# Feed-forward products that take their columns pair by pair in another order, in five of eight chunks

## The chip, the cores and the metric

The kernel runs on one core of a Trainium2 chip. The metric is the device time of one execution in microseconds. Five engines work side by side: TensorE (PE, with its weight loads shown as PEld), VectorE (DVE), ScalarE (ACT), GpSimd (POOL), and SyncE (SP), which issues all DMAs here.

## The reference

Block-local attention with summary keys, followed by a feed-forward layer without a bias. Batch 4, 8 heads, 768 positions, head size 64; model width 512, inner width 2048, 3072 tokens.

```python
k_sum = k.reshape(B, H, nb, 32, D).max(axis=3)
v_sum = v.reshape(B, H, nb, 32, D).mean(axis=3)
scores_l = np.where(abs(pos_q - pos_k) < 16, scale * q @ k.T, -1e9)
scores_s = scale * q @ k_sum.T + log(32)
a = softmax(concatenate([scores_l, scores_s]))
x = (a @ concatenate([v, v_sum])).transpose(0, 2, 1, 3).reshape(3072, 512)
h = x @ w_in
g = where(h >= 1, h, where(h <= -1, 0, (h + 1) ** 2 / 4))
out = g @ w_out
```

## The kernel before

The 3072 tokens are worked in 8 chunks (c) of 384. For each chunk, attention for 4 pairs of heads (p) gives `x` turned: four tiles of 128 model columns by 384 tokens. To keep accuracy, every operand of the feed-forward products is split into a high and a low part in a rounded 32-bit format: `xhi`, `xlo` for `x`, `ghi`, `glo` for the gated inner layer, and `halves` for the weights, whose tiles stay in SBUF for the whole kernel. A product is then three matmuls: high by low, low by high, high by high.

The inner width is walked in 16 steps (f) of 128 columns. A step has these parts:

- `ff1` (L302): 4 pieces (k) of the model width by 3 matmuls, 12 in all, each with 128x128 weights as the stationary operand and 384 token columns of `xhi` or `xlo` as the moving one. All 12 add into one PSUM tile `h` (pool `ps_h`, two buffers).
- the gate (L311 to L329), on ScalarE, VectorE and GpSimd, which writes `ghi` and `glo`.
- `ff2` (L331): 3 groups (i) of 128 tokens by 3 matmuls, 9 in all, with 128x128 of `ghi` or `glo` as the stationary operand and 512 columns of the second weights (`halves`) as the moving one. They add into three PSUM tiles `acc`, one bank each, over all 16 steps.

At the end of a chunk the three `acc` tiles are copied out (L341) and stored (L349).

Chunk 0, with the loading and conversion of the weights, follows an order written out by hand (`OPENING`). From chunk 1 on, a loop gives the order on TensorE: in each step the 12 matmuls of `ff1`, then the 9 of `ff2` of two steps earlier (`LAG` = 2), and every fourth step parts of the attention of the next chunk (scores, transposes, values) between them. The two last `ff2` steps of a chunk fall behind the first `ff1` steps of the next. The other engines follow the waits that result from it.

Of the kernel before, what the change touches and what calls it, by code (L numbers as in the profile page):

```python
# [19 lines left out]
P = 128  # L20
# [7 lines left out]
T = 384  # L28
# [31 lines left out]
FIRST = [[("k", 2), ("q", 2)], [("k", 3), ("q", 3)], [("kraw", 1), ("vraw", 1)], [("kraw", 2), ("vraw", 2)],  # L60
         [("kraw", 3), ("vraw", 3)], [("v", 2), ("v", 3)], [("q", 0), ("q", 1)]]
K_COPY = "vgvg"
HI_POOL = [0, 1, 2, 3, 4, 5, 6, 7, 8, 9, 10, 11, 12, 13, 14, 15]


@with_exitstack
def fused_kernel(ctx: ExitStack, tc: tile.TileContext, q2, kT, kwin, vT, vwin, w_in, w_out, mask, ident, out):
    nc = tc.nc
# [19 lines left out]
    weight, raws, converting, halves = {}, {}, {}, {}  # L88

    def room(i, what, shape, dtype):  # L90

        return wpool.tile(shape, dtype, tag=f"w{i}", name=f"{what}{i}")
# [39 lines left out]
    def convert_high(i):  # L132
        halves[i] = room(i, "halves", [P, 2, 2 * DM], F32R)
        if i in HI_POOL:
            nc.gpsimd.tensor_copy(out=halves[i][:, 0], in_=converting[i].bitcast(F32))
# [13 lines left out]
    def input_tile(pool, what, shape, c, p):  # L149
        if c == 0 and (what, p) in at_first:  # L150
            return at_first[what, p]
        tag, bufs = ("w", W_BUFS) if pool is stage else (what, {"k": K_BUFS, "q": Q_BUFS, "v": 2}[what])
        return pool.tile(shape, F32, tag=tag, name=f"{what}{c}_{p}", bufs=bufs)
# [45 lines left out]
    def window_keys(c, p):  # L199

        k_t = k_ts[c, p] = input_tile(load, "k", [P, NB, KA], c, p)
        eng = {"v": nc.vector, "g": nc.gpsimd}[K_COPY[p]]
        blocks = raws["k", p].rearrange("p (n q) -> p n q", q=QB)
# [95 lines left out]

    hs, ts, gs, acc, outs = {}, {}, {}, {}, {}  # L300

    def ff1(c, f, k):  # L302
        if k == 0:
            hs[c, f] = ps_h.tile([P, 512], F32, tag="h", name=f"h{c}_{f}")
        x_hi, x_lo = xs[c, k]
        for n, (w, x) in enumerate(((1, x_hi), (0, x_lo), (0, x_hi))):
            nc.tensor.matmul(hs[c, f][:, :T], weight["win", f][w][:, k * P:(k + 1) * P], x,  # L307
                             start=(k == 0 and n == 0), stop=(k == NK - 1 and n == 2))


# [20 lines left out]
    def ff2(c, f):  # L331
        if f == 0:
            acc[c] = [ps.tile([P, DM], F32, tag="ps", name=f"acc{c}_{i}") for i in range(NTT)]
        g_hi, g_lo = gs[c, f]
        for i in range(NTT):
            rows = slice(i * P, (i + 1) * P)
            for n, (a, w) in enumerate(((g_lo, 0), (g_hi, 1), (g_hi, 0))):
                nc.tensor.matmul(acc[c][i], a[:, rows], weight["wout", f][w], start=(f == 0 and n == 0),  # L338
                                 stop=(f == NF - 1 and n == 2))

    def result(c, i):  # L341
# [11 lines left out]
    def load_constants():  # L353
# [9 lines left out]
        "T": transposes, "P": turned, "Y": sum_vals, "Z": turn_vals, "V": mean_vals, "W": spread_vals, "A": values, "X": high, "L": low,  # L363
        "a": convert_top, "b": convert_low, "c": convert_join, "d": convert_high, "e": convert_rest,
        "F": ff1, "G": gate_half, "H": gate_square, "I": gate_min, "J": gate_high, "O": gate_rest, "B": ff2, "U": result, "o": store,
    }
    done = set()
# [118 lines left out]
```

## Time and profile before

| | |
|---|---|
| median of 3 runs | 670.58 us (668.12 to 671.68) |
| span of the profiled execution | 670.7 us; no separate time is recorded beside it |
| instructions | 11802 |
| mean granted TensorE clock | 0.982 |
| matmuls of the first product (L307) | 1536, 192 per chunk |
| matmuls of the second product (L338) | 1152, 144 per chunk |

A matmul's duration as shown includes the time in which it overlaps the one before and after it, so the pace of TensorE is read from the distance between starts, or from the chain of waits, not from the mean duration. The trace names tiles without their numbers: `h`, `acc`, `xhi`, `halves` stand for all chunks, and the chunk is found by the time.

### The profile page before, as it was taken

The page shows a single profiled execution, that of the slowest core. Times are in us where ns is not written, and L with a number is a line of the kernel's source. Part 1 is how long each engine was busy: PE and PEld are TensorE (multiplying, and loading weights), DVE is VectorE, ACT ScalarE, POOL GpSimd, SP SyncE. Part 2 cuts the span into 40 slices and gives each one's busy share as a digit, 9 for nine tenths or more (in the row PEclk, how much of TensorE's full clock was granted, in tenths as well). Part 3 has the DMA queues.
Part 4 walks back from the last instruction along what each step waited for, and adds up shares of the span by engine and source line. Part 5 has one row for each costly group of instructions (what it writes and reads, how often), then busy time and mean ns, then how long its engine had stood idle before and what let it go on. Part 6 is the DMA issues. An engine that isn't in the chain of part 4 may idle for free.

```text
span 670.7 us, 11802 instructions
## 1 busy us (share of the span) xinstructions
PE 633.5 (94%) x4448; PEld 559.4 (83%) x4448; DVE 259.4 (39%) x561; ACT 367.5 (55%) x945; POOL 267.1 (40%) x300
## 2 busy tenths in 40 slices
PE   2579998779999999999999999999999999999997
PEld 2478986668888888988888889888888988889996
DVE  5899974642233321245322322336222322311111
ACT  3889745555555545555554554555545645544332
POOL 2589996333332333234333333334233333322221
PEclk9789999879999999999999999999999999999999
DMA  8999703851111401154111311135110200000001
GB/s 285 311 354 323 250 1 85 248 145 52 53 52 53 145 19 35 52 169 124 53 53 48 106 45 52 52 112 181 53 42 11 88 19 19 1 17 32 1 1 47
DMA packets 49768, 63.56 MB, mean 95 GB/s; under 512 B 24880, under 2 KB 33328, under 8 KB 49712
## 3 DMA queue, kind: packets, MB, share of 16 engines
q1 hardware_dynamic: 49712, 62.81, 30.9%
q8 instruction: 35, 0.57, 0.4%
q14 instruction: 21, 0.17, 0.1%
HBM read 56.51 MB, written 6.29 MB: 94 GB/s over the span
## 4 chain that ended last, share of the span: by engine, by line
PE 82%; DMA 7%; ACT 4%; DVE 4%; issue 2%; POOL 1%; SPq 0%; ACTq 0%; DVEq 0%; POOLq 0%
PE h L307 36%; PE acc L338 36%; PE o_ps L286 4%; PE s_ps L242 3%; DMA raw<-in_w_out 3%; PE t_ps L275 3%; DMA raw<-in_w_in 2%; DMA kraw<-in_kT 1%; ACT e L260 1%; DMA first<-in_vT 1%; DMA first<-in_kT 1%; ACT raw L110 1%; DVE c L124 1%; DVE w L130 1%; DVE c L127 1%
## 5 line engine op out<-in xcount | busy, mean ns | idle before, releaser
L307 PE MATMUL h<-xhi,halves 128*128 128x384 f32 x1024 | 285.4, 341 | 5.6 <-DVE t L319 5.5
L338 PE MATMUL acc<-halves,ghi 128*128 128x512 f32 x768 | 240.2, 394 | 0.0
L329 POOL TENSOR_TENSOR glo<-t,ghi 128x384 fp32r<-128x384 f32 x128 | 129.3, 1013 | 200.6 <-ACT ghi L324 194.5
L307 PEld LDWEIGHTS h<-xhi,halves 128*128 128x128 f32 x1024 | 188.5, 189 | 14.1 <-DVE t L319 4.8
L319 DVE SCALAR_TENSOR_TENSOR t<-h,t 128x384 f32<-128x384 f32 x128 | 70.8, 557 | 280.7 <-ACT t L316 268.9
L307 PE MATMUL h<-xlo,halves 128*128 128x384 f32 x512 | 173.3, 338 | 0.0
L338 PEld LDWEIGHTS acc<-halves,ghi 128*128 128x128 f32 x768 | 145.1, 189 | 27.9
L338 PE MATMUL acc<-halves,glo 128*128 128x512 f32 x384 | 154.2, 401 | 0.0
L313 ACT ACTIVATE t<-h,ones_half 128x384 f32<-128x384 f32 x128 | 73.6, 578 | 130.5 <-PE h L307 120.0
L260 ACT ACTIVATE e<-e,den 128x120 f32<-128x120 f32 x192 | 73.3, 383 | 63.8 <-DVE den L255 63.8
L324 ACT CAST ghi<-t 128x384 fp32r<-128x384 f32 x128 | 65.3, 513 | 64.5 <-DVE t L319 64.0
L307 PEld LDWEIGHTS h<-xlo,halves 128*128 128x128 f32 x512 | 96.8, 189 | 4.3 <-DVE xlo L297 0.4
L338 PEld LDWEIGHTS acc<-halves,glo 128*128 128x128 f32 x384 | 72.5, 189 | 12.3 <-issue 1.0
L270 POOL TENSOR_TENSOR e<-e,den 128x360 f32<-128x360 f32 x64 | 49.8, 790 | 61.6 <-DVE den L266 55.8
L316 ACT ACTIVATE t<-t 128x384 f32<-128x384 f32 x128 | 66.8, 525 | 3.7
L214 POOL COPY k<-ks 128x144 f32<-128x144 f32 x30 | 9.2, 310 | 86.4 <-DMA k<-in_kwin 61.1
L143 POOL TENSOR_TENSOR halves<-w,halves 128x1024 fp32r<-128x1024 f32 x16 | 38.6, 2415 | 0.9
L230 POOL COPY v<-v 24x640 f32<-24x640 f32 x30 | 21.5, 717 | 39.7 <-issue 37.2
L286 PEld LDWEIGHTS o_ps<-pt,v 120*64 120x64 f32 x720 | 25.0, 144 | 13.8 <-ACT ghi L324 7.5
L297 DVE TENSOR_TENSOR xlo<-o_ps,xhi 128x384 fp32r<-128x384 f32 x32 | 17.7, 554 | 47.3 <-ACT xhi L292 47.3
L260 ACT ACTIVATION_READ_ACCUMULATOR e<-e,den 128x1 f32 x192 | 35.9, 187 | 0.0
L275 PE MATMUL t_ps<-ident_sb,e 128*120 128x128 f32 x192 | 30.8, 298 | 5.2 <-POOL e L270 5.0
(56 smaller groups left out, 426.4 us busy)
## 6 DMA issues: line engine op xcount, KB each, us to landing
k<-in_kwin SPq DMA_DIRECT2D x28, 360.0 KB, 4.3
v<-in_vwin SPq DMA_DIRECT2D x30, 288.0 KB, 3.1
raw<-in_w_in SPq DMA_DIRECT2D x16, 512.0 KB, 10.8
raw<-in_w_out SPq DMA_DIRECT2D x16, 512.0 KB, 11.0
out<-o SPq DMA_DIRECT2D x24, 256.0 KB, 2.1
q<-in_q SPq DMA_DIRECT2D x56, 96.0 KB, 4.0
kraw<-in_kT SPq DMA_DIRECT2D x13, 384.0 KB, 3.8
vraw<-in_vT SPq DMA_DIRECT2D x13, 384.0 KB, 3.8
```

The lines of the kernel that those rows point to most:

```text
L143: nc.gpsimd.tensor_tensor(out=lo, in0=converting[i].bitcast(F32), in1=hi.bitcast(F32), op=ALU.subtract)
L260: nc.scalar.activation(out=e[:, t, :], in_=e[:, t, :], func=AF.Exp, bias=nm[:, t:t + 1], scale=1.0, accum_out=den[:, t:t + 1])
L270: nc.gpsimd.tensor_tensor(out=e, in0=e, in1=den.unsqueeze(2).broadcast_to([P, NT, KA]), op=ALU.mult)
L275: nc.tensor.transpose(t_pss[c, p, j][:KA, t * P:(t + 1) * P], es[c, p, j][:, t, :], ident_sb)
L286: nc.tensor.matmul(o_pss[c, p][j * D:(j + 1) * D, cols], v_ts[c, p][:KA, blk, j * D:(j + 1) * D], pts[c, p, j][:KA, cols], start=True, sto ...
L307: nc.tensor.matmul(hs[c, f][:, :T], weight["win", f][w][:, k * P:(k + 1) * P], x, start=(k == 0 and n == 0), stop=(k == NK - 1 and n == 2))
L313: nc.scalar.activation(out=ts[c, f], in_=hs[c, f][:, :T], func=AF.Relu, bias=ones_half, scale=0.5)
L316: nc.scalar.square(out=ts[c, f], in_=ts[c, f])
L319: nc.vector.scalar_tensor_tensor(out=ts[c, f], in0=hs[c, f][:, :T], scalar=1.0, in1=ts[c, f], op0=ALU.max, op1=ALU.min)
L324: nc.scalar.copy(out=hi, in_=ts[c, f])
L329: nc.gpsimd.tensor_tensor(out=lo, in0=ts[c, f], in1=hi.bitcast(F32), op=ALU.subtract)
L338: nc.tensor.matmul(acc[c][i], a[:, rows], weight["wout", f][w], start=(f == 0 and n == 0), stop=(f == NF - 1 and n == 2))
```

## The change

In chunks 2, 3 and 4 the matmuls of `ff1`, and in chunks 5 and 6 those of `ff2`, take the columns of their moving operand in another order, and write them to PSUM in the same other order, so every sum lands where it did before. The columns are cut into `count` equal blocks; pairs of two adjacent columns stay together, and the matmul takes the first pair of every block, then the second pair of every block, and so on.

| chunk | product | blocks | distance from one pair to the next |
|---|---|---|---|
| 2 | `ff1`, 384 columns | 2 | 192 columns (768 bytes), then back |
| 3 | `ff1` | 24 | 16 columns (64 bytes) |
| 4 | `ff1` | 12 | 32 columns (128 bytes) |
| 5 | `ff2`, 512 columns | 32 | 16 columns (64 bytes) |
| 6 | `ff2` | 2 | 256 columns (1024 bytes), then back |

A column is one 4-byte value in each partition. Stationary operands, waits, buffers and the order of the instructions on every engine stay as they are; the same number of matmuls stands in the same places, with shapes such as 128x96x2x2 in place of 128x384.

```diff
+STRIDED_1 = {2: 2, 3: 24, 4: 12}
+STRIDED_2 = {5: 32, 6: 2}
...
+    def strided(ap, count):
+
+        return ap if count is None else ap.rearrange("p (a b w) -> p b a w", a=count, w=2)
+
     def ff1(c, f, k):
...
-            nc.tensor.matmul(hs[c, f][:, :T], weight["win", f][w][:, k * P:(k + 1) * P], x,
+            nc.tensor.matmul(strided(hs[c, f][:, :T], STRIDED_1.get(c)), weight["win", f][w][:, k * P:(k + 1) * P],
+                             strided(x, STRIDED_1.get(c)),
                              start=(k == 0 and n == 0), stop=(k == NK - 1 and n == 2))
...
-                nc.tensor.matmul(acc[c][i], a[:, rows], weight["wout", f][w], start=(f == 0 and n == 0),
+                nc.tensor.matmul(strided(acc[c][i], STRIDED_2.get(c)), a[:, rows],
+                                 strided(weight["wout", f][w], STRIDED_2.get(c)), start=(f == 0 and n == 0),
                                  stop=(f == NF - 1 and n == 2))
```

## The prediction

> **What bounds the kernel now.** I read the page first, for the share of each engine and the granted clock.
>
> ```profile
> PE 633.5 (94%) x4448; PEld 559.4 (83%) x4448; DVE 259.4 (39%) x561; ACT 367.5 (55%) x945; POOL 267.1 (40%) x300
> ...
> PE   2579998779999999999999999999999999999997
> ...
> PEclk9789999879999999999999999999999999999999
> ...
> PE 82%; DMA 7%; ACT 4%; DVE 4%; issue 2%; POOL 1%; SPq 0%; ACTq 0%; DVEq 0%; POOLq 0%
> PE h L307 36%; PE acc L338 36%; PE o_ps L286 4%; PE s_ps L242 3%; DMA raw<-in_w_out 3%; PE t_ps L275 3%; DMA raw<-in_w_in 2%; DMA kraw<-in_kT 1%; ACT e L260 1%; DMA first<-in_vT 1%; DMA first<-in_kT 1%; ACT raw L110 1%; DVE c L124 1%; DVE w L130 1%; DVE c L127 1%
> ```
>
> TensorE is busy in 94% of the span, and the two feed-forward products are 36% each of the chain that ended last. A busy PE need not be PE at its peak, so I cut the span at the stores of the output. They come three to a chunk, once per 77 us.
>
> ```profile
> 217.43 1.63 SPq L350 DMA_DIRECT2D out<-o  x3
> 294.50 1.63 SPq L350 DMA_DIRECT2D out<-o  x3
> ...
> 525.69 1.63 SPq L350 DMA_DIRECT2D out<-o  x3
> ```
>
> The busy time of each engine in these stretches follows (columns: stretch, its length, then busy time and count of PE, PEld, DVE, ACT, POOL; granted clock; DMA share; GB/s). The store of chunk c-1 opens the stretch that holds the 192 matmuls of L307 of chunk c.
>
> ```profile
> 217.43:294.50 77.07, 77.07 (x558) 68.61 (x557) 23.43 (x56) 41.72 (x114) 26.51 (x31) 1.00 0.23 66
> 294.50:371.56 77.06, 77.06 (x558) 68.59 (x557) 27.13 (x60) 41.68 (x114) 26.95 (x35) 1.00 0.29 87
> 371.56:448.63 77.07, 77.07 (x558) 68.61 (x557) 23.43 (x56) 41.71 (x114) 25.73 (x30) 1.00 0.23 66
> 448.63:525.69 77.06, 77.06 (x558) 68.59 (x557) 27.29 (x60) 41.62 (x114) 27.18 (x35) 1.00 0.28 84
> 525.69:601.98 76.29, 76.29 (x534) 67.99 (x533) 19.17 (x46) 39.34 (x102) 23.79 (x26) 1.00 0.06 19
> ```
>
> These are chunks 2 to 6, the five that the change touches. PE has no idle time in any of them, its clock is granted in full, and no other engine passes 42 us of 77. So PE's own pace sets the end there: a nanosecond more per matmul is a nanosecond more on the end, and a wait of another engine that became shorter would bring nothing.
>
> The pace is read from starts, since a matmul's shown duration (about 340 and 395 ns) overlaps its neighbours. Each row below is start, time and count of a group.
>
> ```profile
> 230.79 0.34 PE L307 MATMUL h<-xlo,halves 128*128 128x384 f32 x1
> ...
> 232.53 0.34 PE L307 MATMUL h<-xhi,halves 128*128 128x384 f32 x1
> 232.70 0.39 PE L338 MATMUL acc<-halves,glo 128*128 128x512 f32 x1
> ...
> 233.39 0.39 PE L338 MATMUL acc<-halves,glo 128*128 128x512 f32 x1
> ```
>
> Eleven matmuls of 384 columns start in 232.70 - 230.79 = 1.91 us, 174 ns each; three of 512 columns in 233.39 - 232.70 = 0.69 us, 230 ns each. The 128 columns between them cost 56 ns, 0.44 ns per column, which leaves about 5 ns per matmul that do not depend on columns. The chain of waits gives the same per step:
>
> ```profile
> 221.96 2.08 PE acc L338 x9
> 224.03 2.09 PE h L307 x12
> 226.12 0.11 PE vs_ps L222
> 226.23 0.66 PE t_ps L275 x6
> ```
>
> **The change, part by part.** Nothing is added, removed or moved: the same instructions stand on each queue in the same order, and only the column order inside some matmuls differs. No wait, no buffer and no DMA changes, so queues, releases and the other four engines need no term unless PE's pace changes.
>
> First products. Chunks 2, 3 and 4 have 16 steps of 12 matmuls, at 2.09 us a step (the row at 224.03): 33.4 us a chunk, 100.3 us for 576 matmuls. They now take their columns two by two with jumps: in chunk 2 to and fro between halves 192 columns (768 bytes) apart, in chunk 3 with a step of 16 columns (64 bytes), in chunk 4 of 32 columns (128 bytes).
>
> Second products. Chunks 5 and 6 have 16 steps of 9 matmuls at 2.08 us (the row at 221.96): 33.3 us a chunk, 66.6 us for 288 matmuls. Chunk 5 steps by 16 columns, chunk 6 to and fro between halves 256 columns (1024 bytes) apart.
>
> Together 166.9 us of the span, a quarter of it, run in another order. The cost is 166.9 us times the relative slowdown of a column, and the trace of before has no TensorE row that reads or writes in jumps, so I bound it from both sides.
>
> From below: the number of columns is the same, and 0.44 ns per column is what a run of adjacent columns takes at a clock granted in full. A gain could only come from the 5 ns per matmul: 864 x 5 ns = 4 us. Nothing in the edit takes an instruction away, so I set the gain at nothing and keep 4 us as the outer end.
>
> From above: the slowest pace at which PE takes columns in a run in this stretch is that of the transposes at 226.23, 0.66 us / 6 = 110 ns for 128 columns, 0.86 ns per column, against 2.09 us / 12 / 384 = 0.454 ns. That is 1.90 times as long; all five chunks at that pace cost 0.90 x 166.9 = 150 us.
>
> Between these ends, two kinds of row are near. For a read in jumps: VectorE reads every second word of the raw weights at L124, and adjacent words of PSUM at L344.
>
> ```profile
> L124 DVE TENSOR_SCALAR c<-raw 128x512 int32<-128x512 int32 x32 | 20.5, 684 | 2.4 <-ACT raw L110 2.4
> ...
> L344 DVE COPY o<-acc 128x512 f32<-128x512 f32 x8 | 5.5, 682 | 3.6 <-PE acc L338 3.6
> ```
>
> Both take 512 elements, in 684 and 682 ns: a pattern that uses two of every four words cost VectorE nothing, at 1.3 ns per element, three times PE's time per column. It is weak evidence, as its memory and pace differ, but it is the only row with gaps, and it stands at the lower end. For interference: PE's pace is not perfectly steady. In another part of the same chunk, with the same tiles and the clock still full, a step takes longer:
>
> ```profile
> 273.37 2.12 PE h L307 x12
> 275.49 2.10 PE acc L338 x9
> ```
>
> That is 1.4% and 1.0%, so something that the profile does not name can take a hundredth of the pace. If the new order made that the rule in the five stretches, it would cost 0.03 x 48 + 0.02 x 32 = 2.1 us, under what can be measured.
>
> I take nothing. The reason beside the VectorE rows: the change keeps each pair of neighbours together, so every second column still follows its neighbour as before, and only the place of the next pair is new. The sum is 670.7 + 0 = 670.7 us against the span of the profiled execution, for which the page gives no time beside its span. The median of the three runs is 670.58 and their spread is 668.12 to 671.68, 0.5%, about what a measurement of this kernel can tell from no change. I give 670.6.
>
> [...]
>
> **Rivals.** One: a jump between pairs costs TensorE, whatever its length, on the read of the moving operand or on the write of the sum. Place: every matmul of the five stretches, on a PE with no idle time in them. It decides from 3.4 us (0.5% of 670.7), 3.4 / 166.9 = 2% of a matmul: 3.5 ns of 174. At the pace of the transposes it gives 670.7 + 150 = 821 us. For it: PE is the only bound, and a pair lasts only 2 x 0.44 = 0.9 ns, the shortest time in which any memory here has to deliver. Against it: the VectorE rows. Three of the chunks could be spared or only two hit, which is the next.
>
> Two: only some step lengths cost, because pairs at certain distances meet in the same part of a memory. All five distances are multiples of 64 bytes, so such a meeting is possible in any, and they differ enough that one may hit and another not. A chunk that is hit at the transposes' pace costs 0.90 x 33.4 = 30 us: 701 us for one, 731 for two. For it: two of the chunks swing between two places and three walk in even steps, so they load the memories differently. Against it: no row shows such a dependence.
>
> Three: a small loss, by more meetings of the moving read with the weight load that runs beside it (PEld is busy 68.6 us of each 77). The priced sign is the 1.4% above; three to six times that, 4 to 8%, gives 7 to 13 us: 678 to 684 us. For it: the loads use the same memory and already overlap. Against it: the pace in the main part of the chunk repeats to 0.01 us in every chunk although DMA share and the load of the other engines vary (0.06 to 0.29).
>
> Four: a gain out of the 5 ns, at most 4 us: 667 us. I see no mechanism for it.
>
> **How the numbers follow.** No change 0.58; small loss 0.10; some chunks hit 0.15; all hit 0.15; a gain 0.02. Slower by over 0.5% holds the three losses, 0.40. The likeliest case is 670.6, alone 667 to 674. Two in ten may be left out: no change, the small loss and most of the case of one or two chunks are inside up to 733 us, while the all-hit case, the gain, and a few in a hundred of the rest lie outside. The range is 667 to 733.
>
> **What would show it.** Right: stores still 77.07 us apart through chunks 2 to 5 and 76.29 in chunk 6, and steps of 2.08 to 2.12 us in all of them. Wrong: a stretch that has grown, with PE still busy all the time, and by its number the chunk says which step length does it: the stretches that start at 217, 294 and 371 for the first products, the two last for the second ones. If the first three grow and the last two do not, or the reverse, the order hurts only with one product's operands. Chunks 1 and 7, which are untouched, must keep their pace; if they lose too, it is the clock and not the order. What makes the forecast wrong is one fact: that TensorE needs more than a pair in one place.

## The result, and the profile after

The changed kernel takes 790.8 us (median of 4 runs, 789.87 to 791.73) against 671.13 us before: 1.178 times as long (95% interval 1.174 to 1.182). The forecast of no change was wrong, and the time lies above its range.

The page of the changed kernel, engines and granted clock:

```profile
PE 751.6 (95%) x4448; PEld 579.8 (74%) x4448; DVE 260.0 (33%) x561; ACT 369.1 (47%) x945; POOL 266.7 (34%) x300
...
PEclk9699998899999999999999999999999999999999
```

PE's busy time grew from 633.5 to 751.6 us, by the 118 us that the span grew (670.7 to 788.7); that of its weight loads grew by 20 (559.4 to 579.8). VectorE, ScalarE and GpSimd were busy within 2 us of what they were, and waited more. Cut at the stores as before, the five stretches (columns as in the prediction) are:

```profile
219.20:311.23 92.03, 92.03 (x558) 72.61 (x557) 23.53 (x56) 41.80 (x114) 25.41 (x29) 1.00 0.19 55
311.23:418.15 106.92, 106.92 (x558) 74.60 (x557) 26.68 (x60) 42.09 (x114) 27.01 (x35) 1.00 0.21 63
418.15:522.98 104.83, 104.83 (x558) 74.14 (x557) 23.41 (x56) 42.12 (x114) 25.36 (x29) 1.00 0.16 49
522.98:628.06 105.08, 105.08 (x554) 70.62 (x553) 27.96 (x60) 41.80 (x115) 27.10 (x35) 1.00 0.20 62
628.06:719.29 91.23, 91.23 (x534) 69.17 (x533) 19.11 (x45) 39.43 (x102) 23.73 (x26) 1.00 0.05 16
```

PE is still busy all the time, at a clock granted in full, and the stretches are 15.0, 29.9, 27.8, 28.0 and 14.9 us longer, 115.5 us in all. For the first products a stretch runs from one step into its chunk to one step into the next, so the growth of a stretch is not quite that of a chunk. The chain of waits gives one step of each chunk's changed product, in the order of the chunks 2 to 6 and last the untouched chunk 7:

```profile
245.25 2.97 PE h L313 x12
...
342.26 3.96 PE h L313 x12
...
449.07 3.96 PE h L313 x12
...
554.20 3.89 PE acc L345 x9
...
657.03 2.95 PE acc L345 x9
...
735.08 2.08 PE h L313 x12
```

Against 2.09 and 2.08 us before, the patterns with 24, 12 and 32 blocks cost 1.87 to 1.90 times as much, and the two that swing between two halves 1.42 times. The product that was left alone in each chunk kept its pace (2.08 us for `acc` at 248.22, 346.22 and 459.80; 2.09 to 2.12 for `h` in chunks 5 and 6), and so did chunk 7. So it is not the clock, and the price depends on the pattern.

### The profile page after: what moved, and what is told of

Its sections match the earlier page's. It is cut to its first block, busy times and chain, and to the rows that moved or that the text cites. A ratio compares the mean times of both kernels' runs of the same rounds, so it can differ in the third digit from the quotient of the medians.

```text
span 788.7 us, 11796 instructions
## 1 busy us (share of the span) xinstructions
PE 751.6 (95%) x4448; PEld 579.8 (74%) x4448; DVE 260.0 (33%) x561; ACT 369.1 (47%) x945; POOL 266.7 (34%) x300
## 4 chain that ended last, share of the span: by engine, by line
PE 88%; DMA 6%; SPq 3%; ACT 1%; DVE 1%; issue 0%; POOL 0%; POOLq 0%; DVEq 0%; ACTq 0%
PE h L313 42%; PE acc L345 38%; PE o_ps L288 3%; PE s_ps L244 3%; DMA raw<-in_w_in 2%; PE t_ps L277 2%; DMA raw<-in_w_out 2%; SPq L189 1%; DMA first<-in_q 1%; DMA vraw<-in_vT 1%; SPq L103 1%; DMA out<-o 1%; ACT raw L117 0%; PE vs_ps L224 0%; ACT e L262 0%
## 5 line engine op out<-in xcount | busy, mean ns | idle before, releaser
L313 PE MATMUL h<-xhi,halves 128*128 128x384 f32 x1024 | 337.7, 394 | 6.5 <-DVE t L326 6.5
L345 PE MATMUL acc<-halves,ghi 128*128 128x512 f32 x768 | 270.4, 435 | 0.0
L313 PEld LDWEIGHTS h<-xhi,halves 128*128 128x128 f32 x1024 | 195.7, 194 | 52.3 <-issue 5.4
L313 PE MATMUL h<-xlo,halves 128*128 128x384 f32 x512 | 200.2, 391 | 0.0
L345 PEld LDWEIGHTS acc<-halves,ghi 128*128 128x128 f32 x768 | 147.5, 192 | 53.3 <-issue 18.6
L320 ACT ACTIVATE t<-h,ones_half 128x384 f32<-128x384 f32 x128 | 73.8, 579 | 235.4 <-PE h L313 225.3
L345 PE MATMUL acc<-halves,glo 128*128 128x512 f32 x384 | 169.9, 442 | 0.0
L313 PEld LDWEIGHTS h<-xlo,halves 128*128 128x128 f32 x512 | 99.3, 194 | 21.7 <-issue 2.9
L288 PE MATMUL o_ps<-pt,v 120*64 120x64 f32 x720 | 30.1, 238 | 4.5 <-ACT first L228 4.5
```

The source lines that it names most:

```text
L288: nc.tensor.matmul(o_pss[c, p][j * D:(j + 1) * D, cols], v_ts[c, p][:KA, blk, j * D:(j + 1) * D], pts[c, p, j][:KA, cols], start=True, sto ...
L313: nc.tensor.matmul(strided(hs[c, f][:, :T], STRIDED_1.get(c)), weight["win", f][w][:, k * P:(k + 1) * P], strided(x, STRIDED_1.get(c)), st ...
L320: nc.scalar.activation(out=ts[c, f], in_=hs[c, f][:, :T], func=AF.Relu, bias=ones_half, scale=0.5)
L345: nc.tensor.matmul(strided(acc[c][i], STRIDED_2.get(c)), a[:, rows], strided(weight["wout", f][w], STRIDED_2.get(c)), start=(f == 0 and n ...
```

## The experiments

In the experiments a pattern is written (blocks, columns kept together): (24,2) is the change's chunk 3. A step is 12 matmuls of 384 columns (first product) or 9 of 512 (second), 2.08 us when plain.

**Read or write.** The change alters the order of two accesses at once: the read of the moving operand in SBUF and the write of the sums in PSUM. Each was undone by itself.

```diff
-            nc.tensor.matmul(strided(hs[c, f][:, :T], STRIDED_1.get(c)), ...
+            nc.tensor.matmul(hs[c, f][:, :T], ...
-                nc.tensor.matmul(strided(acc[c][i], STRIDED_2.get(c)), a[:, rows],
+                nc.tensor.matmul(acc[c][i], a[:, rows],
```

> Only the moving operand is read in the new order in the five chunks; PSUM is written in the plain order, so the columns of the result come out permuted within those chunks. Read theory (the jumps cost where the moving operand is read): all of the loss stays, steps of 2.97, 3.96 and 3.96 us for the first products of chunks 2, 3, 4 and 3.89 and 2.95 us for the second products of chunks 5 and 6, in all about 790 us. Write theory (the jumps cost where the sums go into PSUM): nothing stays, steps of 2.09 and 2.08 us, about 671 us. If both sides cost together: something between, in the same chunks.

Measured: 790.71 us, ratio to before 1.172 (1.168 to 1.177). The stretches of chunks 2, 3 and 6:

```profile
220.35:312.37 92.02, 92.02 (x558) 72.60 (x557) 23.43 (x56) 41.81 (x114) 25.40 (x29) 1.00 0.19 55
312.37:419.30 106.93, 106.93 (x558) 74.62 (x557) 26.69 (x60) 42.15 (x114) 27.00 (x35) 1.00 0.22 63
...
629.21:720.44 91.23, 91.23 (x534) 69.18 (x533) 19.11 (x45) 39.42 (x102) 23.74 (x26) 1.00 0.05 16
```

They agree with the changed kernel's to 0.01 us.

```diff
-                             strided(x, STRIDED_1.get(c)),
+                             x,
-                                 strided(weight["wout", f][w], STRIDED_2.get(c)), start=(f == 0 and n == 0),
+                                 weight["wout", f][w], start=(f == 0 and n == 0),
```

> Only the output is written in the new order in the five chunks; the moving operand is read in the plain order, so the columns of the result come out permuted within those chunks. Read theory: steps of 2.09 and 2.08 us as before, about 671 us. Write theory: steps of 2.97, 3.96, 3.96 us (first products) and 3.89, 2.95 us (second products), about 790 us. If the slower of two sides sets the pace and both are slow, this run and the one with the reads alone are both near 790 us.

Measured: 672.64 us, ratio 0.9996 (0.997 to 1.002). All five stretches:

```profile
219.51:296.58 77.07, 77.07 (x558) 68.61 (x557) 23.55 (x56) 41.70 (x114) 26.42 (x31) 1.00 0.22 66
296.58:373.65 77.07, 77.07 (x558) 68.60 (x557) 26.97 (x60) 41.65 (x114) 27.13 (x35) 1.00 0.29 87
373.65:450.71 77.06, 77.06 (x558) 68.59 (x557) 23.47 (x56) 41.69 (x114) 25.70 (x30) 1.00 0.23 66
450.71:527.78 77.07, 77.07 (x558) 68.61 (x557) 27.77 (x60) 41.69 (x114) 27.20 (x35) 1.00 0.27 84
527.78:604.07 76.29, 76.29 (x534) 67.99 (x533) 19.19 (x46) 39.37 (x102) 23.81 (x26) 1.00 0.06 19
```

The read theory holds: the read of the moving operand is the whole loss, and writing pairs in jumps to PSUM costs nothing at any of the five distances, to 0.01 us a stretch.

**Which distance, which length.** As each chunk has two products, one kernel can hold 14 patterns. From here on only the read is altered.

```diff
-STRIDED_1 = {2: 2, 3: 24, 4: 12}
-STRIDED_2 = {5: 32, 6: 2}
+STRIDED_1 = {1: (3, 2), 2: (4, 2), 3: (6, 2), 4: (8, 2), 5: (64, 2), 6: (32, 2), 7: (16, 2)}
+STRIDED_2 = {1: (4, 2), 2: (8, 2), 3: (16, 2), 4: (64, 2), 5: (128, 2), 6: (2, 4), 7: (32, 4)}
...
-        return ap if count is None else ap.rearrange("p (a b w) -> p b a w", a=count, w=2)
+        return ap if order is None else ap.rearrange("p (a b w) -> p b a w", a=order[0], w=order[1])
```

> Reads only, output written in plain order (its columns come out permuted). Each chunk has its own pattern, as (blocks, columns kept together). First products, chunks 1 to 7: (3,2), (4,2), (6,2), (8,2) with far jumps, then pairs 24, 48 and 96 bytes apart. Second products, chunks 1 to 7: (4,2), (8,2), (16,2), pairs 32 and 16 bytes apart, then (2,4) and (32,4), four columns kept together. Time of a step, 2.08 us when plain. Line theory (each visit to another 16-byte line costs the time of four adjacent columns): all pairs 16 to 96 bytes apart 3.9 to 4.0; (2,4) and (32,4) stay 2.08, since four values fill a line; the few-block patterns 3.96 too unless some lines are kept, as (2,2) with its 2.97 hints. Jump theory (a fixed two columns' time for each jump within the inner loop of the pattern, none for the step back): (3,2) 3.4, (4,2) 3.5, (6,2) 3.7, (8,2) 3.8; 24, 48 and 96 bytes 3.9; (2,4) 2.6 and (32,4) 3.1. Meeting theory (only jumps by a multiple of 64 bytes cost): 16, 24, 32, 48 bytes 2.08, the far ones 3.4 to 3.96, 96 bytes about 3.

The line of 16 bytes in the first theory is an assumption at this point; the cells that bear on its size come with the two lanes below.

One execution each of this kernel and of the two after it took 1080.25, 807.55 and 850.65 us; they are read by their steps. Steps from the chain of waits: (3,2), (4,2), pairs 24 bytes apart, pairs 16 bytes apart, and (2,4); then pairs 96 bytes apart, and two steps of (32,4).

```profile
168.85 3.39 PE h L313 x12
...
310.24 4.02 PE h L313 x12
...
760.59 4.08 PE h L313 x12
...
737.61 4.08 PE acc L345 x9
...
870.88 2.26 PE acc L345 x9
...
939.02 5.61 PE h L313 x12
...
983.68 3.64 PE acc L345 x9
...
992.92 2.03 PE acc L345 x9
```

Pairs cost about the same at 16, 24, 32 (4.15) and 48 bytes (4.04) as at 64, so the meeting theory falls. (4,2), (6,2) and (8,2) are at 4.02, 4.06 and 3.92, (3,2) at 3.39. The line theory is right on pairs, with (3,2) as a case in which some lines are kept, and nearly on (2,4). Two cells fit no theory: pairs 96 bytes apart took 5.61 us, and (32,4), beside them in the same chunk, varied between 2.03 and 3.64.

```diff
+STRIDED_1 = {1: (192, 1), 2: (96, 1), 3: (2, 4), 4: (48, 4), 5: (2, 8), 6: (24, 8), 7: (12, 16)}
+STRIDED_2 = {1: (2, 1), 2: (256, 1), 3: (128, 1), 4: (32, 8), 5: (16, 16), 6: (64, 4), 7: (8, 32)}
```

> Reads only, output written in plain order (its columns come out permuted). First products, chunks 1 to 7, as (blocks, columns kept together): (192,1) and (96,1), single columns 8 and 16 bytes apart; (2,4), (48,4); (2,8), (24,8); (12,16). Second products: (2,1), to and fro between halves; (256,1) and (128,1), single columns 8 and 16 bytes apart; (32,8), (16,16), (64,4), (8,32). Line theory: (192,1) 4.0 and (256,1) 3.9, two values of each line; (96,1) and (128,1) 7.9, one value of each; every pattern that keeps 4, 8, 16 or 32 aligned columns together 2.08. Jump theory: two columns' time for each jump: (192,1), (96,1), (256,1), (128,1) all about 6; (48,4) and (64,4) 3.1; (24,8) and (32,8) 2.6; (12,16) and (16,16) 2.3; (8,32) 2.2; (2,4) 2.6, (2,8) 2.3. Meeting theory: single columns 8 and 16 bytes apart 2.08, (24,8) 2.3, (48,4) and (64,4) 2.08.

Steps of (192,1), (96,1), (48,4), (24,8), and (2,1):

```profile
177.07 4.08 PE h L313 x12
...
286.79 4.16 PE h L313 x12
...
526.72 2.12 PE h L313 x12
...
680.19 2.08 PE h L313 x12
...
175.13 1.95 PE acc L345 x9
```

Four or more adjacent columns are at or near the plain pace in this run, whatever the distance (2.08 to 2.20 us, only (2,4) at 2.35), so the jump theory falls. But the line theory falls as well: single columns 16 bytes apart, each on its own line, cost 4.16 and not 7.9, the same as two values per line (4.08). And (2,1), which jumps 1024 bytes at every column, was the fastest of all, 1.95 against 2.06 plain.

**Two lanes.** The new theory: odd and even columns of the stream are fetched side by side, in two lanes, and a lane keeps pace only if it finds two values in a row on one 16-byte line. In a plain read each lane sees columns 0, 2 | 4, 6: two per line. In pairs with jumps it sees one per line. In (2,1) one lane walks through the first half and the other through the second. The rival is that a run of four adjacent columns is what counts. They part where columns are not adjacent, yet each lane has two per line, and where four are adjacent but straddle two lines.

```diff
+ORDER_1 = {1: (2, 1, 1), 2: (12, 1, 1), 3: (4, 1, 1), 4: (6, 1, 1), 5: (2, 2, 1), 6: (2, 4, 1), 7: "near"}
+ORDER_2 = {2: (16, 2, 1), 3: (32, 1, 4), 4: (32, 1, 4), 5: (2, 2, 1), 6: (4, 1, 1), 7: (8, 1, 1)}
+SHIFT_2 = {1: 2, 3: 2}
...
+        if order == "near":
+            return ap.rearrange("p (g a b) -> p g b a", a=2, b=16)
+        a, s, w = order
+        if s == 1:
+            return ap.rearrange("p (a b w) -> p b a w", a=a, w=w)
+        return ap.rearrange("p (a b s) -> p s b a", a=a, s=s)
```

> Reads only, output written in plain order (its columns come out permuted; a shifted read takes other columns). First products, chunks 1 to 7: (2,1), (12,1), (4,1) and (6,1), single columns from so many blocks in turn; two blocks in turn with steps of 8 and of 16 bytes within each; two blocks only 64 bytes apart in turn. Second products: plain but started 8 bytes into a line (chunk 1); single columns from 16 blocks with steps of 8 bytes (2); (32,4) started 8 bytes into a line (3); (32,4) (4); two blocks in turn with steps of 8 bytes (5); (4,1) (6); (8,1) (7). Two-lane theory (the odd and the even columns of the stream are fetched side by side, and each of the two goes at full pace only if it finds two values in a row on one 16-byte line): first products 1.95, 3.96, about 2.9, about 3.4, 1.95 to 2.08, 3.96, 1.95; second products 2.07, 3.9 to 4.1, 3.9 to 4.1, 2.1, 1.95 to 2.08, about 2.9, 3.9 to 4.1. Adjacent-run theory (full pace only where at least four columns are adjacent, with two blocks in turn as an exception): the two-block reads with a step of 8 bytes are slow, 3.96 and 3.9, and (32,4) shifted stays at 2.1; single columns from 4 or 6 blocks are 3.96.

First products: two blocks with steps of 8 bytes, and of 16 bytes, then (2,1), two blocks 64 bytes apart, (4,1), (6,1):

```profile
573.91 2.12 PE h L322 x12
...
664.54 4.09 PE h L322 x12
...
157.94 1.95 PE h L322 x12
...
765.53 1.95 PE h L322 x12
...
390.62 2.45 PE h L322 x12
...
512.34 2.79 PE h L322 x12
```

Second products, (32,4) started 8 bytes into a line, and (32,4) on whole lines:

```profile
402.14 4.03 PE acc L355 x9
...
510.34 2.00 PE acc L355 x9
```

The two-lane theory has the right side in every cell in which the two differ. Steps of 8 bytes in two streams, with no two neighbours adjacent, run at the plain pace, and steps of 16 bytes at half of it. Four adjacent columns run at half pace once they are moved by 8 bytes, so that each lane finds one value per line. What the runs show is a pattern of the cells tried: where each column shares an aligned block of 16 bytes with the column two places before or behind it in the stream, a step took 1.95 to 2.35 us, (32,4) beside the pairs at 96 bytes excepted; elsewhere 2.45 to 5.61. The size of the block is read from the cells just named: steps of 8 bytes in two streams 2.12 and of 16 bytes 4.09, (32,4) on whole blocks 2.00 and moved by 8 bytes 4.03. A line means such a block here. The two lanes are the author's picture of this; no trace shows them. And the picture does not explain the two cells at 96 bytes above.

The prices between can be estimated from the step times by the same picture. From the 1.95 us of undisturbed lanes to the 3.96 of (24,2) are 2.01 us for 12 x 192 = 2304 visits of a lane to a new line: 0.87 ns for each visit that finds one value. In (2,2) a lane alternates between two lines of two values each: 2.97 - 1.95 = 1.02 us for 1152 lines, 0.89 ns a line, so by this estimate each line is paid for once and its second visit is free. In (4,1) it alternates between two lines of four values: 0.50 us for 576 lines, 0.87 ns. With three lines in turn ((3,2) 3.39, (6,1) 2.79) part of the second visits is paid, with four ((4,2) 4.02) all. That two lines are kept is a reading of these numbers, not shown by itself. It was expected in part only: (4,1) and (6,1) came out cheaper than the 2.9 and 3.4 written down, and (8,1), at 4.46, dearer than 3.9 to 4.1.

**A faster version.** If two streams are faster than plain reads (1.95 against 2.06 us in the second product above), both products should read two streams in all chunks. To get plain results out, the columns of the second weights are laid out beforehand as even and odd halves, and the token order that comes out of the first product is undone by the store.

```diff
+    def two_streams(ap):
+        return ap.rearrange("p (a b) -> p b a", a=2)
...
-            nc.tensor.matmul(hs[c, f][:, :T], weight["win", f][w][:, k * P:(k + 1) * P], x,
+            nc.tensor.matmul(hs[c, f][:, :T], weight["win", f][w][:, k * P:(k + 1) * P], two_streams(x),
-                nc.tensor.matmul(acc[c][i], a[:, rows], weight["wout", f][w], start=(f == 0 and n == 0),
+                nc.tensor.matmul(acc[c][i], a[:, rows], two_streams(weight["wout", f][w]), start=(f == 0 and n == 0),
-        nc.sync.dma_start(out=out[c * T + i * P:c * T + (i + 1) * P, :], in_=outs[c, i])
+        rows = out[c * T:(c + 1) * T, :].rearrange("(a b) d -> b a d", a=2)[i * P // 2:(i + 1) * P // 2]
+        nc.sync.dma_start(out=rows, in_=outs[c, i])
...
+    arrays["w_out"] = np.ascontiguousarray(np.concatenate([w_out[:, 0::2], w_out[:, 1::2]], axis=1)).view(np.uint64)
```

> A version that gives the reference's result: in all chunks both products read their moving operand as single columns of the two halves in turn, and write in plain order; the columns of the second weights are laid out for that beforehand, and the token order is undone by the store. Two-lane theory: matmuls of 384 columns in about 162 ns in place of 176, of 512 in 216 in place of 232: 1536 x 14 + 1152 x 16 = 40 us less, some of it not seen in chunk 0, where other engines are waited for: about 635 us, ratio 0.94 to 0.96. If the 216 ns that (2,1) showed was peculiar to that chunk: 671 us.

Measured: 653.76 us, ratio 0.972 (0.968 to 0.976). From chunk 1 on the steps are 1.95 and 1.94 us, as expected, but only 20 us were won and not 40; the ratio lies above the expected 0.94 to 0.96. The stretches shrank (72.63 us between the last two rows below, against 77.07), but the opening took longer. The first store is at 123.55 us (112.61 before, and 112.6 to 116.4 over all seven kernels so far with a plain chunk 0):

```profile
123.55 0.61 SPq L355 DMA_DIRECT2D out<-o  x1
...
223.68 2.02 SPq L355 DMA_DIRECT2D out<-o  x3
296.31 2.02 SPq L355 DMA_DIRECT2D out<-o  x3
```

The groups by line show what became slow there, first ScalarE's row of before, then the two rows of this version that correspond to it and to the L124 row in the prediction:

```profile
L110 ACT ACTIVATE raw<-raw 128x1024 f32<-128x1024 f32 x16 | 17.7, 1153 | 1.2 <-DMA raw<-in_w_in 1.2
```

```profile
L124 DVE TENSOR_SCALAR c<-raw 128x512 int32<-128x512 int32 x32 | 24.4, 826 | 3.1 <-ACT raw L110 3.1
```

```profile
L110 ACT ACTIVATE raw<-raw 128x1024 f32<-128x1024 f32 x16 | 22.3, 1495 | 2.0 <-DMA raw<-in_w_in 1.9
```

These read every second word of the raw weights (L110 also writes it back in place), and only while chunk 0 runs. Reads of adjacent words kept their time (L320, the square of the gate on ScalarE, 524 ns against 525 at L316 before). So the reads with gaps may be disturbed by the two streams. The chain of waits says so too: two instructions of L124 in a row took 1.74, 1.50 and 1.44 us in it, at 54.74, 98.05 and 102.31, against 1.19 to 1.20 in all five such pairs of before. That was tested from both sides: two streams in all chunks but 0, and in chunk 0 alone.

```diff
-        return ap.rearrange("p (a b) -> p b a", a=2)
+        return ap.rearrange("p (a b) -> p b a", a=2) if c else ap
```

> As the version with two streams in all chunks, and with the reference's result, but chunk 0 reads in plain order (its output columns are put right in the copy out). Interference theory: the two-stream reads of chunk 0 slowed the reads with gaps of VectorE and ScalarE in the conversion of the weights (L124 826 ns in place of 684, L110 1495 in place of 1153); without them these rows are back at 684 and 1153 and the first store at about 113 to 116 us in place of 123.6, so about 644 us, ratio 0.95 to 0.96. Rival (the late opening came from the laid-out weights or from chance): the first store stays at 123, 653 us.

Measured: 643.47 us, ratio 0.957 (0.953 to 0.961). The first store, one stretch between stores, and the two rows:

```profile
111.71 0.37 SPq L359 DMA_DIRECT2D out<-o  x1
```

```profile
210.54:283.17 72.63, 72.63 (x557) 66.47 (x557) 23.43 (x56) 41.34 (x114) 25.88 (x30) 1.00 0.24 70
```

```profile
L124 DVE TENSOR_SCALAR c<-raw 128x512 int32<-128x512 int32 x32 | 20.5, 686 | 1.9 <-ACT raw L110 1.9
```

```profile
L110 ACT ACTIVATE raw<-raw 128x1024 f32<-128x1024 f32 x16 | 17.8, 1157 | 0.8 <-DMA raw<-in_w_in 0.6
```

```diff
+        return ap if c else ap.rearrange("p (a b) -> p b a", a=2)
```

> Only chunk 0 reads its moving operands as two streams; its tokens and columns come out permuted. Interference theory: L124 about 826 ns, L110 about 1495 ns, first store about 123 us in place of 112.6, all later chunks 77.06 us apart: 670 + 8 to 11 = about 680 us, though PE's matmuls in chunk 0 are faster (162 and 216 ns). Rival: the rows of L124 and L110 as before and a first store at or before 112.6 us, 668 us.

Measured: 683.25 us in one run, beside a median of 672.7 for the kernel before on the same chip.

```profile
123.91 0.38 SPq L354 DMA_DIRECT2D out<-o  x1
```

```profile
L124 DVE TENSOR_SCALAR c<-raw 128x512 int32<-128x512 int32 x32 | 24.0, 800 | 3.5 <-ACT raw L110 3.5
```

```profile
L110 ACT ACTIVATE raw<-raw 128x1024 f32<-128x1024 f32 x16 | 22.9, 1516 | 2.2 <-DMA raw<-in_w_in 2.2
```

The interference theory holds on both sides: rows and store follow the streams of chunk 0 (111.71 us without them, 123.55 and 123.91 with them), and the plain weights of the second run rule out the laid-out ones as the cause. The version with two streams from chunk 1 on is the fastest of all, 4.3% under the kernel before.

## Why the prediction was wrong

- **What bounds the kernel.** Right: PE has no idle time in the five stretches, so its pace came out in the span one for one. The time that ScalarE's first gate instruction waited for `h` grew from 120 to 225 us in all and cost nothing.
- **The size of the part that is touched.** Right: 166.9 us. The steps give 16 x (0.88 + 1.87 + 1.87) + 16 x (1.81 + 0.87) = 117 us of extra time, and the span grew by 118.
- **The bounds.** Neither was a bound. That the dearest patterns of the change cost 1.90 times as much, the figure taken from the transposes, is luck: no run ties the two together, and pairs 96 bytes apart cost 5.61 / 2.09 = 2.7 times. The lower end fell too, though not for this change: a pattern exists that is faster than plain, 1.95 against 2.08 us. The 5 ns per matmul were set as all that could be gained; two streams won 174 - 162 = 12 and 230 - 216 = 14 ns per matmul. The step took 0.44 ns as what a column must cost; two streams show (216 - 162.5) / 128 = 0.42, from 1.94 us / 9 and 1.95 us / 12.
- **The step that failed** is "I take nothing", with its reason that pairs stay together and only the place of the next pair is new. The runs showed in its place that the read of the moving operand in jumping pairs adds 42 to 90% to a plain step, 117 us in all, and the write nothing. The VectorE rows on which the choice leaned show 1.3 ns per element, TensorE takes a column in 0.44. By the two-lane theory a pair is one value for each lane, the very case in which no lane finds a second value on its line. The caution in the text, that memory and pace differ, should have weighed more than the row: a row of another engine was no bound for this one.
- **The rivals.** The first, a jump costs at any length on the read or the write, was nearest: every changed chunk slowed, 791 us against its 821. It was too high since the two patterns with two blocks add 42% to a step and not 90%. Of its two places the read is shown and the write is excluded. The second, that the distance decides, is refuted for 16 to 64 bytes (3.89 to 4.15 us a step), though 96 and 256 bytes cost more than the rest (5.61 and 4.39); the split that it pointed at, two chunks that swing and three that walk, is the one measured (1.42 against 1.87 to 1.90). The third, a loss of 4 to 8%, and the fourth, a gain, are refuted by the size.

## What to carry to other kernels

The order in which a matmul reads its moving operand was a cost of its own here: for 4-byte columns, runs of four that fill whole 16-byte blocks took 2.00 to 2.35 us a step (one pattern up to 3.64), two separate runs in turn 1.94 to 1.95, and pairs with jumps 2.95 to 5.61; so keep such runs, or feed two in turn, and try no jumps after pairs without a measurement. The order of the writes, in pairs, was free at the five distances tried (ratio 0.9996). Where TensorE has no idle time, reading two streams in turn is worth trying (ratio 0.957 here), but look at what other engines read with gaps at that time (684 to 826 ns on VectorE here). When a trace has no row of the engine in question, the bounds should carry the forecast, not a row of another engine.

## What the runs showed of the hardware

- Two streams in turn make 384 columns in 162 ns and 512 in 216 (1.95 us / 12 and 1.94 / 9); plain reads take 174 and 230. Why plain reads are 7% slower is not settled. The two streams with steps of 8 bytes give each lane of the picture two values per line, as a plain read does, and were back at the plain pace (2.08 to 2.12 us), so what counts may be the number of values per line; no run was made for that. The 1.4% waver within a chunk that the prediction quotes is gone in the kernels with two streams (most steps 1.94 or 1.95 us, where before had 2.06 to 2.12).
- Two streams in chunk 0 slowed reads with gaps on VectorE (684 to 826 ns) and ScalarE (1153 to 1495 ns); the square of the gate, which reads adjacent words, was not slowed (525 to 524 ns). Where the two meet is open.
- Some distances cost more than a missed line: pairs 96 bytes apart 5.61 us a step, pairs or single columns 256 bytes apart ((8,2) and (8,1) of 512) 4.39 and 4.46, where others take 3.9 to 4.2. And (32,4) was at 2.00 to 2.10 in one kernel and wavered up to 3.64 beside the pairs at 96 bytes. Nothing here explains this.
